# Sparse attention and two gated stages on one core: four of nine transposed score banks split on ScalarE with a subtracting matmul, v of the last keys padded by DMA

## The chip, the core and the metric

The kernel runs on one core of a Trainium2 chip, as one program. The metric is the device time of one execution in microseconds (us); 1231.96 us is the median of three executions (1230.54 to 1233.79).

## What is computed

```python
scores = scale * np.matmul(q, k.transpose(0, 1, 3, 2))      # (4, 8, 576, 576), head size 64
thresh = np.max(scores, axis=-1, keepdims=True) - tau
scores = np.where(scores >= thresh, scores, -1e9)
attn = np.exp(scores - np.max(scores, axis=-1, keepdims=True))
attn = attn / (np.sum(attn, axis=-1, keepdims=True) + 1e-09)
x = np.matmul(attn, v)                 # then tokens x 512: 2304 x 512
g = x @ w_gate
x = (silu(g) * (x @ w_val)) @ w_out    # d_ff 1536
out = ((x @ w1) * (x @ w2) @ w3) @ w_out2   # d_ff 1024
```

All inputs are float32 or float64 (the weights come as 64-bit words and are converted on the chip).

## The kernel before

Every product has float32 accuracy from a faster matmul type: an operand is split into a high part `hi`, rounded to the type fp32r, and a low part `lo` = value − hi, and products of the parts are added up in PSUM. Much of the work of the other engines is the making of these pairs.

**Attention.** Two heads of a batch make a pair; there are 16 pairs, and a pair has nine score tiles of 128 queries by 576 keys (four of each head, and a ninth for the last 64 queries of both). For a tile TensorE makes the scores in an `s_bank` (L428, two such banks), VectorE copies them out negated with a running minimum (L467), ScalarE takes the exponential (L476), GpSimd adds tau to the statistic (L459) and VectorE masks and sums (L486, in place in the tile `P`, from the two SBUF tensors `P` and `E`). Then TensorE transposes the masked scores into a `t_bank` (PSUM, 512 columns, four such banks, shared with all other transposes and the outputs of attention). A pair has ten such banks: four of each head (`it_T`, L523), one for the last queries (`it_lq`, L529) and one for the last keys (`it_kl`, L540). Each is split into hi and lo by `evac_split` before TensorE multiplies it with v (`it_pv`, L565 and L570).

**The split.** `evac_split` takes the next letter of a string for each bank. X: ScalarE copies the bank to hi (L499), and VectorE subtracts hi from the bank (L501). Y: ScalarE copies the bank to an SBUF tile (L512), and GpSimd casts (L99) and subtracts (L102). W: ScalarE copies twice (L512, L516), and GpSimd subtracts (L517). X's second step is put off until the next work item has been issued (`deferred`, emptied by `run_item`).

```python
PATHS, LAST = "XYWYXYWYXY", "XW"     # ten letters, ten banks of a pair; LAST for the last pair
```

**v of the last keys.** `VLZ` holds, for each head of a pair, hi and lo of v for the 64 last keys in the 64 partitions of that head, with zeros in the others. `split_v` fills it for each pair with four small GpSimd operations (L99 and L102 on `VLZ`).

**Order.** `some` takes items of the pair from a list (`main`) between the tiles, about 2.2 items for a tile; the build then places the instructions of each engine by its own model of time, so that the order on an engine isn't that of the code. SyncE issues all transfers, in order.

**After attention.** The first gated stage starts while the last pair is still under way: `x_prep` loads attention's output again (`x_dram`, L770) and the reciprocal sums (`r_dram`, L774), adds on GpSimd (L805), scales on VectorE (L808) and splits (L796, L797). From then on the matmuls of the two gated stages (L814) follow on TensorE until the end. Weights are converted in between (L127 to L156).

Of the kernel before, what the change touches and what calls it, by code (L numbers as in the profile page):

```python
# [24 lines left out]
N_TMP, N_BIG, N_HB, N_TA = 6, 3, 3, 3  # L25
# [4 lines left out]
PATHS, LAST = "XYWYXYWYXY", "XW"  # L30
# [5 lines left out]
def kernel(  # L36
# [47 lines left out]
    ident_r = const.tile([P, P], F32R, name="ident_r")  # L84
    tau_sb = const.tile([P, 1], F32, name="tau_sb")
# [141 lines left out]
    def attention(actx, early, tail):  # L227
# [30 lines left out]
        def load_left(b):  # L258
            qk = ld.tile([P, H, D], F32, tag="qkl", name="qkl", bufs=1)
            vl = wk.tile([P, HP, D], F32, tag="vl", name="vl", bufs=2)  # L260
            nc.sync.dma_start(out=qk[0:64], in_=q[b, :, 512:S, :].rearrange("h p d -> p h d"))
            nc.sync.dma_start(out=qk[64:128], in_=k[b, :, 512:S, :].rearrange("h p d -> p h d"))
            vs = v[b, :, 512:S, :].rearrange("(g e) p d -> e p g d", e=2)
            for e in range(2):
                nc.sync.dma_start(out=vl[64 * e:64 * e + 64], in_=vs[e])
            lraw[b] = (qk, vl)
# [17 lines left out]
        def split_left(b):  # L284
# [11 lines left out]
            lsplit[b] = (qks, vl)  # L296

        def split_v(p):
# [4 lines left out]
            vl = lsplit[p // HP][1]  # L303
            for h in range(2):
                r = slice(64 * h, 64 * h + 64)
                vz = VLZ[r, p % 2, h]
                split_pool(vz[:, 0, :], vz[:, 1, :], vl[r, p % HP, :])
# [187 lines left out]
        def evac_split(hi, lo, bank):  # L495
            path = LAST[path_i[0] % len(LAST)] if in_tail else PATHS[path_i[0] % len(PATHS)]
            path_i[0] += 1
            if path == "X":
# [19 lines left out]

        def it_T(p, h, c):
            bank = t_bank()  # L520
            for t in range(4):
                o = 640 * h + c * P
                nc.tensor.transpose(bank[:, t * P:(t + 1) * P], pbuf[p, t][:, o:o + P], ident)  # L523
            evac_split(AT[h][:, 0, c, 0:512], AT[h][:, 1, c, 0:512], bank)

        def it_lq(p):
            bank = t_bank()
            for c in range(4):
                nc.tensor.transpose(  # L529
                    bank[:, c * P:(c + 1) * P], pbuf[p, 4][:, c * P:(c + 1) * P], ident  # L530
                )
# [5 lines left out]
        def it_kl(p):  # L537
            bank = t_bank()
            for t in range(4):
                nc.tensor.transpose(bank[:, t * P:(t + 1) * P], pbuf[p, t][:, 512:640], ident)  # L540
            evac_split(ATL[:, 0, 0:512], ATL[:, 1, 0:512], bank)
# [196 lines left out]
    nc.vector.tensor_copy(out=ident_r, in_=ident)  # L738

# [363 lines left out]
```

## Time and profile before

| | |
|---|---|
| median of three executions | 1231.96 us |
| the profiled execution: its time, its span | 1231.65 us, 1229.9 us |
| TensorE matmul busy | 1114.0 us (91%) |
| VectorE busy | 788.0 us (64%) |
| ScalarE busy | 563.0 us (46%) |
| GpSimd busy | 604.7 us (49%) |
| mean granted TensorE clock | 0.971 |

PE is TensorE's matmul, PEld its weight load, DVE VectorE, ACT ScalarE, POOL GpSimd, SP SyncE. Busy time is a mean over stages with different limits, so a change to one stage is read in that stage. An "idle before" is the time in which an engine stood ahead of an instruction, with the instruction that ended it.

### The profile page before, as it was taken

To read this page: it belongs to the slowest core of one execution; us is meant where nothing else is said; L and a number is where in the kernel's file an instruction comes from. 1 tells how busy PE (TensorE), PEld (TensorE's weight loads), DVE (VectorE), ACT (ScalarE), POOL (GpSimd) and SP (SyncE) were. 2 spreads that over 40 slices of the span, in tenths; PEclk is the share of its full clock that TensorE was granted. 3 is DMA by queue.
4 is the path that set the end of the run, shared out by engine and by line. 5 is a ranking of instruction groups with operands and counts; after the bars stand their busy time and mean duration, and the time that the engine had idled before them with its cause. 6 is when DMAs were issued, how large, how long until landed. Compare 5 with 4: busy or idle time off the path is not lost.

```text
span 1229.9 us, 16704 instructions
## 1 busy us (share of the span) xinstructions
PE 1114.0 (91%) x5972; PEld 952.0 (77%) x5972; DVE 788.0 (64%) x1303; ACT 563.0 (46%) x1010; POOL 604.7 (49%) x602
## 2 busy tenths in 40 slices
PE   7888878888777845999999999999999999999998
PEld 5877777778666644888888888888877888888886
DVE  7999999999988635756546373548795021432223
ACT  6777667777755522634234242335474241231211
POOL 7999989999975423533323142324342131231110
PEclk9999999999978967999999999999999999999999
DMA  9856656555444544321102021113431010000014
GB/s 203 202 134 148 146 132 149 129 131 133 106 133 134 140 118 131 103 69 52 53 18 69 18 69 52 52 35 103 127 107 58 1 35 1 18 18 1 1 52 103
DMA packets 104370, 107.07 MB, mean 87 GB/s; under 512 B 47328, under 2 KB 78688, under 8 KB 104288
## 3 DMA queue, kind: packets, MB, share of 16 engines
q1 hardware_dynamic: 104288, 106.01, 33.2%
q8 instruction: 47, 0.77, 0.3%
q14 instruction: 35, 0.29, 0.1%
HBM read 68.16 MB, written 14.23 MB: 67 GB/s over the span
## 4 chain that ended last, share of the span: by engine, by line
PE 55%; DVE 15%; POOL 13%; DMA 8%; issue 3%; SPq 3%; ACT 1%; DVEq 0%; POOLq 0%; ACTq 0%
PE t_bank L814 36%; PE s_bank L814 18%; DVE P L486 5%; POOL AT L102 4%; DMA slot<-r_dram 3%; DVE P L467 3%; POOL AT L99 3%; DMA raw<-in_moe_w_gate_dram 2%; POOL AT L517 2%; DMA raw<-in_moe_w_dram 2%; POOL stat L459 2%; SPq L770 1%; DVE tmp L156 1%; DVE slot L797 1%; DVE tmp L144 1%
## 5 line engine op out<-in xcount | busy, mean ns | idle before, releaser
L814 PE MATMUL t_bank<-slot,slot 128*128 128x512 f32 (+1 forms) x2592 | 566.3, 374 | 25.2 <-ACT slot L796 14.1
L814 PEld LDWEIGHTS t_bank<-slot,slot 128*128 128x128 f32 x2592 | 461.4, 191 | 113.2 <-ACT slot L796 14.7
L486 DVE SCALAR_TENSOR_TENSOR P<-P,stat,E 128x576 f32<-128x576 f32 x144 | 184.2, 1303 | 1.6 <-POOL stat L459 1.3
L814 PE MATMUL s_bank<-h,slot 128*128 128x512 f32 (+1 forms) x720 | 163.6, 376 | 16.6 <-POOL h L106 15.6
L149 POOL TENSOR_TENSOR raw<-raw 128x512 int32<-128x512 int32 x76 | 86.9, 1144 | 159.7 <-ACT raw L148 149.2
L814 PEld LDWEIGHTS s_bank<-h,slot 128*128 128x128 f32 x720 | 128.7, 194 | 40.9 <-POOL h L106 16.5
L1043 POOL TENSOR_TENSOR h<-tmp,h 128x512 fp32r<-128x512 f32 (+1 forms) x38 | 45.8, 1204 | 200.5 <-ACT h L1041 200.5
L106 POOL TENSOR_TENSOR h<-tmp,h 128x512 fp32r<-128x512 f32 (+1 forms) x60 | 73.5, 1225 | 136.5 <-ACT h L105 136.4
L1039 DVE TENSOR_TENSOR tmp<-tmp,t_bank 128x512 f32<-128x512 f32 (+1 forms) x40 | 25.3, 633 | 178.3 <-PE t_bank L814 178.3
L476 ACT ACTIVATE E<-P,stat 128x576 f32<-128x576 f32 x144 | 112.6, 789 | 54.6 <-DVE P L467 27.9
L428 PE MATMUL s_bank<-R,L 128*128 128x288 f32 x512 | 100.3, 318 | 28.9 <-DVE P L467 24.8
L467 DVE TENSOR_SCALAR_CACHE_REDUCE P<-s_bank,neg 128x576 f32<-128x576 f32 x144 | 114.0, 806 | 5.1 <-PE s_bank L428 4.9
L899 DVE TENSOR_TENSOR tmp<-tmp,t_bank 128x512 f32<-128x512 f32 (+1 forms) x60 | 37.9, 631 | 116.7 <-PE t_bank L814 112.9
L814 PE MATMUL s_bank<-slot,h 128*128 128x512 f32 x432 | 106.6, 391 | 0.9 <-DVE slot L1029 0.8
L565 PE MATMUL t_bank<-AT,sp 128*128 128x288 f32 x512 | 94.2, 312 | 13.5 <-POOL AT L102 7.9
L428 PEld LDWEIGHTS s_bank<-R,L 128*128 128x128 f32 x512 | 74.9, 193 | 39.1 <-DVE P L467 34.6
L814 PEld LDWEIGHTS s_bank<-slot,h 128*128 128x128 f32 x432 | 80.0, 188 | 18.3 <-DVE slot L1029 2.1
L898 ACT ACTIVATE tmp<-t_bank 128x512 f32<-128x512 f32 (+1 forms) x60 | 33.3, 555 | 128.1 <-PE t_bank L814 125.3
L565 PEld LDWEIGHTS t_bank<-AT,sp 128*128 128x128 f32 x512 | 76.3, 195 | 19.0 <-POOL AT L102 11.2
L861 DVE TENSOR_TENSOR slot<-s_bank,slot 128x1024 f32<-128x1024 f32 (+1 forms) x68 | 77.6, 1142 | 18.6 <-PE s_bank L814 16.5
L523 PE MATMUL t_bank<-ident,P 128*128 128x128 f32 x512 | 75.7, 282 | 10.0 <-ACT AT L516 2.5
L156 DVE SCALAR_TENSOR_TENSOR tmp<-tmp,raw 128x512 f32<-128x512 f32 x76 | 66.6, 876 | 26.6 <-POOL raw L149 26.6
(105 smaller groups left out, 1511.4 us busy)
## 6 DMA issues: line engine op xcount, KB each, us to landing
raw<-in_moe_w_dram SPq DMA_DIRECT2D x32, 512.0 KB
raw<-in_moe_w_out_dram SPq DMA_DIRECT2D x20, 512.0 KB
x_dram<-xs SPq DMA_DIRECT2D x64, 144.0 KB
L<-qhi SPq DMA_DIRECT2D x60, 128.0 KB
L<-qlo SPq DMA_DIRECT2D x60, 128.0 KB
raw<-in_moe_w_gate_dram SPq DMA_DIRECT2D x12, 512.0 KB
raw<-in_moe_w_val_dram SPq DMA_DIRECT2D x12, 512.0 KB
ld<-in_k_dram SPq DMA_DIRECT2D x16, 256.0 KB
```

Of the source, the lines that this page charges most:

```text
L102: nc.gpsimd.tensor_tensor(out=lo, in0=src, in1=f32(hi), op=ALU.subtract)
L106: nc.gpsimd.tensor_tensor(out=lo, in0=src, in1=f32(hi), op=ALU.subtract)
L149: nc.gpsimd.tensor_tensor(out=a, in0=a, in1=x, op=ALU.subtract)
L156: nc.vector.scalar_tensor_tensor(out=f32(m), in0=f32(m), scalar=2.0 ** 20, in1=f32(a), op0=ALU.add, op1=ALU.mult)
L428: nc.tensor.matmul(o, lhsT=lhs, rhs=R[:, c:c + HALF], start=(h == hs2[0] and e == 0), stop=(h == hs2[-1] and e == 1),)
L467: nc.vector.tensor_scalar(out=p_tile(p, i).rearrange("p (a c) -> p a c", a=2), in0=sb[:, :, 0:HALF], scalar1=neg, scalar2=None, op0=ALU.mu ...
L476: nc.scalar.activation(out=e, in_=p_tile(p, i), func=ACTF.Exp, scale=-1.0, bias=stats[p // HP][:, 0, c:c + 1],)
L486: nc.vector.scalar_tensor_tensor(out=t, in0=t, scalar=stats[b][:, 1, c:c + 1], in1=e, op0=ALU.is_le, op1=ALU.mult, accum_out=sums[b][:, c: ...
L523: nc.tensor.transpose(bank[:, t * P:(t + 1) * P], pbuf[p, t][:, o:o + P], ident)
L565: nc.tensor.matmul(o, lhsT=vs[:, 4 * h + c, :, :].rearrange("p a d -> p (a d)"), rhs=AT[h][:, e, c, cs], start=(c == 0 and e == 0), stop=F ...
L814: nc.tensor.matmul(o, lhsT=lhs(a), rhs=rhs(c), start=(first and i == 0), stop=(last and i == 2))
L861: nc.vector.tensor_tensor(out=a, in0=s, in1=a, op=ALU.add)
```

## The change

Three things are changed, all in the attention part.

1. The letters are now nine for ten banks, so that they move round from pair to pair: `"XZYXZZYXZ"`, and `"XZ"` for the last pair. W is gone. Z is new: ScalarE copies the bank to hi; TensorE multiplies hi with minus the identity (`minus_r`) into the same bank, so that the bank then holds value − hi; ScalarE copies the bank to lo. The last two steps are put off until the next item, as X's second step is. In all 160 banks there were 51 X, 72 Y and 37 W; there are now 56 X, 32 Y and 72 Z. The transposes of a bank are issued as one accumulation group (`turn_p`), so that a further matmul can add to it.
2. v of the last keys is split once for a batch into `vls` (two GpSimd operations of 128x256, for four pairs), and two transfers a pair on SyncE's queue move 64 partitions of it into `VLZ`.
3. The pool of extra SBUF tiles for Y has one buffer in place of three (`N_TA`), and the raw v of the last keys one in place of two.

```diff
-N_TMP, N_BIG, N_HB, N_TA = 6, 3, 3, 3
+N_TMP, N_BIG, N_HB, N_TA = 6, 3, 3, 1
-PATHS, LAST = "XYWYXYWYXY", "XW"
+PATHS, LAST = "XZYXZZYXZ", "XZ"
+    minus_r = const.tile([P, P], F32R, name="minus_r")
-            vl = wk.tile([P, HP, D], F32, tag="vl", name="vl", bufs=2)
+            vl = ld.tile([P, HP, D], F32, tag="vl", name="vl", bufs=1)
@@ split_left
-            lsplit[b] = (qks, vl)
+            vls = wk.tile([P, HP, 2, D], F32R, tag="vls", name="vls", bufs=2)
+            split_pool(vls[:, :, 0, :], vls[:, :, 1, :], vl)
+            lsplit[b] = (qks, vls)
@@ split_v
-            vl = lsplit[p // HP][1]
+            vls = lsplit[p // HP][1]
             for h in range(2):
                 r = slice(64 * h, 64 * h + 64)
-                vz = VLZ[r, p % 2, h]
-                split_pool(vz[:, 0, :], vz[:, 1, :], vl[r, p % HP, :])
+                nc.sync.dma_start(out=f32(VLZ[r, p % 2, h]), in_=f32(vls[r, p % HP]))
@@ evac_split
-            if path == "X":
+            if path == "Z":
+                nc.scalar.copy(out=hi, in_=bank)
+
+                def rest():
+                    nc.tensor.matmul(bank, lhsT=minus_r, rhs=hi, start=False, stop=True,
+                                     skip_group_check=True)
+                    nc.scalar.copy(out=lo, in_=bank)
+
+                deferred.append(rest)
+            elif path == "X":
+        def turn_p(bank, parts):
+            for t, part in enumerate(parts):
+                nc.tensor.matmul(
+                    bank[:, t * P:(t + 1) * P], lhsT=part, rhs=ident, is_transpose=True,
+                    start=(t == 0), stop=(t == len(parts) - 1),
+                )
@@ it_T (it_lq and it_kl in the same way)
-            for t in range(4):
-                o = 640 * h + c * P
-                nc.tensor.transpose(bank[:, t * P:(t + 1) * P], pbuf[p, t][:, o:o + P], ident)
+            o = 640 * h + c * P
+            turn_p(bank, [pbuf[p, t][:, o:o + P] for t in range(4)])
+    nc.vector.tensor_scalar(out=minus_r, in0=ident, scalar1=-1.0, scalar2=None, op0=ALU.mult)
```

Line numbers move a little in the changed kernel: L470 is L467 of before, L489 is L486, L431 is L428, L462 is L459, L101 and L104 are L99 and L102, L331 is L328 (transposes of k and q), L534 stands for all transposes of scores, L505 is the new matmul, L824 is L808.

On TensorE, in the second head's part of a pair, before (L523 transposes of scores, L428 the next tiles' scores):

```order
L523 MATMUL t_bank<-ident,P_976 128x128 [waits Activation_49]
L523 MATMUL t_bank<-ident,P_977 128x128
L523 MATMUL t_bank<-ident,P_978 128x128
L523 MATMUL t_bank<-ident,P_979 128x128
L428 MATMUL s_bank<-R,L 128x288 [waits DVE_49]
L428 MATMUL s_bank<-R,L 128x288 x3
L428 MATMUL s_bank<-R,L 128x288 [waits DVE_49]
L428 MATMUL s_bank<-R,L 128x288 x3
```

and with the change, at the like place:

```order
L534 MATMUL t_bank<-ident,P_964 128x128 [waits DVE_49]
L534 MATMUL t_bank<-ident,P_965 128x128
L534 MATMUL t_bank<-ident,P_966 128x128
L534 MATMUL t_bank<-ident,P_967 128x128
L331 MATMUL t_bank<-ident,ld_987 128x128 [waits Activation_49]
L331 MATMUL t_bank<-ident,ld_987 128x128 x3
L534 MATMUL t_bank<-ident,P_964 128x128 [waits DVE_49]
L534 MATMUL t_bank<-ident,P_965 128x128
L534 MATMUL t_bank<-ident,P_966 128x128
L534 MATMUL t_bank<-ident,P_967 128x128
L505 MATMUL t_bank<-AT,minus_r 128x512 [waits Activation_49]
L431 MATMUL s_bank<-R,L 128x288 [waits DVE_49]
```

The subtracting matmul of the first bank comes after two other groups of transposes and ahead of the next scores, and waits there for ScalarE's copy.

On GpSimd, in the middle of attention, about one pair before (`sp` is v of the pair):

```order
L99 TENSOR_SCALAR VLZ<-vl 64x64
L459 TENSOR_SCALAR stat<-stat,tau_sb 128x2
L99 TENSOR_SCALAR AT<-tmp 128x512
L102 TENSOR_TENSOR VLZ<-vl,VLZ 64x64
L102 TENSOR_TENSOR AT<-tmp,AT 128x512
L99 TENSOR_SCALAR sp_2715<-ld_2119 128x8x64
L99 TENSOR_SCALAR VLZ<-vl 64x64
L517 TENSOR_TENSOR AT<-tmp,AT 128x512
L102 TENSOR_TENSOR sp_2715<-ld_2119,sp_2715 128x8x64
L102 TENSOR_TENSOR VLZ<-vl,VLZ 64x64
L99 TENSOR_SCALAR AT<-tmp 128x512
L459 TENSOR_SCALAR stat<-stat,tau_sb 128x2 x2
```

and with the change, from the v of one pair to that of the next:

```order
L101 TENSOR_SCALAR sp_3533<-ld_2958 128x8x64
L104 TENSOR_TENSOR sp_3533<-ld_2958,sp_3533 128x8x64
L101 TENSOR_SCALAR AT<-tmp 128x512
L104 TENSOR_TENSOR AT<-tmp,AT 128x512
L462 TENSOR_SCALAR stat<-stat,tau_sb 128x2 x2
L101 TENSOR_SCALAR AT<-tmp 128x4x2x64
L462 TENSOR_SCALAR stat<-stat,tau_sb 128x1
L104 TENSOR_TENSOR AT<-tmp,AT 128x4x2x64
L462 TENSOR_SCALAR stat<-stat,tau_sb 128x2 x2
L101 TENSOR_SCALAR sp_3829<-ld_3247 128x8x64
L104 TENSOR_TENSOR sp_3829<-ld_3247,sp_3829 128x8x64
```

A whole pair now has two banks on GpSimd, and nothing on `VLZ`.

On VectorE, in the last pair, where the first gated stage's x is prepared, before (L808 scales x with sums that a transfer brings; the row of `P_4524` is the last of this pair's nine L467):

```order
L467 TENSOR_SCALAR P_4523,stat<-s_bank,neg 128x576 [waits PE_49]
L138 TENSOR_SCALAR tmp<-raw 128x512
L467 TENSOR_SCALAR P_4524,stat<-s_bank,neg 128x576 [waits PE_49]
L808 TENSOR_TENSOR tmp<-tmp,slot_4638 128x512 [waits DMAHW5_49,Pool_49]
L141 TENSOR_SCALAR raw<-raw 128x512 [waits DVE_49]
```

and with the change:

```order
L470 TENSOR_SCALAR P_4433,stat<-s_bank,neg 128x576 [waits PE_49]
L824 TENSOR_TENSOR tmp<-tmp,slot_4545 128x512 [waits DMAHW7_49,Pool_49]
L513 TENSOR_TENSOR ATL<-t_bank,ATL 128x512 [waits Activation_49]
L470 TENSOR_SCALAR P_4434,stat<-s_bank,neg 128x576 [waits PE_49]
```

The wait for such a transfer now stands earlier in the last pair, after its third L470.

## Rows read from the trace of the kernel before

**Rows 1.** Busy time by stretch, the whole core; (x) counts instructions.
```profile
core 0: us, PE busy (x) PEld busy (x) DVE busy (x) ACT busy (x) POOL busy (x), PEclk, DMA share, GB/s
0.00:46.00 46.00, 35.71 (x236) 30.69 (x237) 38.75 (x93) 32.00 (x62) 37.07 (x50) 1.00 0.95 207
46.00:309.00 263.00, 220.67 (x1623) 201.56 (x1621) 259.77 (x516) 188.14 (x377) 250.22 (x286) 0.99 0.61 140
309.00:374.00 65.00, 47.48 (x265) 40.91 (x264) 56.46 (x104) 38.67 (x74) 50.38 (x49) 0.84 0.46 116
374.00:480.00 106.00, 68.70 (x316) 55.95 (x316) 65.56 (x85) 45.58 (x79) 49.02 (x40) 0.81 0.50 141
480.00:1230.00 750.00, 741.48 (x3540) 622.90 (x3538) 367.47 (x510) 258.64 (x420) 218.00 (x180) 1.00 0.17 51
575.00:600.00 25.00, 25.00 (x112) 20.71 (x111) 15.45 (x18) 10.71 (x17) 10.14 (x9) 1.00 0.22 64
```
**Rows 2.** Groups by line and form, 46 to 309 us, VectorE's two main ones.
```profile
L486 DVE SCALAR_TENSOR_TENSOR P<-P,stat,E 128x576 f32<-128x576 f32 x110 | 143.8, 1332 | 1.6 <-POOL stat L459 1.3
L467 DVE TENSOR_SCALAR_CACHE_REDUCE P<-s_bank,neg 128x576 f32<-128x576 f32 x109 | 86.2, 805 | 1.8 <-PE s_bank L428 1.7
```
**Rows 3.** Timeline of VectorE and GpSimd, three masks and what GpSimd did beside them.
```profile
110.24 0.81 DVE L486 SCALAR_TENSOR_TENSOR P<-P,stat,E 128x576 f32<-128x576 f32 x1
111.05 0.63 POOL L99 TENSOR_SCALAR AT<-raw 128x512 fp32r<-128x512 f32 x1 [1.35 <-ACT raw L512]
...
124.16 1.26 POOL L102 TENSOR_TENSOR AT<-tmp,AT 128x512 fp32r<-128x512 f32 x1
124.25 1.79 DVE L486 SCALAR_TENSOR_TENSOR P<-P,stat,E 128x576 f32<-128x576 f32 x1
```
**Rows 4.** Groups by line and form, 46 to 309 us: GpSimd's splits.
```profile
L102 POOL TENSOR_TENSOR AT<-tmp,AT 128x512 fp32r<-128x512 f32 x39 | 55.8, 1437 | 0.4
L99 POOL TENSOR_SCALAR AT<-tmp 128x512 fp32r<-128x512 f32 x39 | 29.9, 769 | 1.7 <-ACT tmp L512 1.1
L102 POOL TENSOR_TENSOR AT<-raw,AT 128x512 fp32r<-128x512 f32 x21 | 29.7, 1418 | 0.2
L517 POOL TENSOR_TENSOR AT<-tmp,AT 128x512 fp32r<-128x512 f32 x16 | 22.1, 1378 | 0.2
L99 POOL TENSOR_SCALAR AT<-raw 128x512 fp32r<-128x512 f32 x22 | 17.2, 784 | 1.8 <-ACT raw L512 1.4 <-DMA x_dram<-xs 0.5
L99 POOL TENSOR_SCALAR VLZ<-vl 64x64 fp32r<-64x64 f32 x24 | 13.8, 577 | 1.0
L102 POOL TENSOR_TENSOR VLZ<-vl,VLZ 64x64 fp32r<-64x64 f32 x24 | 12.7, 529 | 1.0
L517 POOL TENSOR_TENSOR AT<-raw,AT 128x512 fp32r<-128x512 f32 x8 | 11.8, 1469 | 0.2
```
**Rows 5.** The same view: a VectorE subtraction of X and a ScalarE copy.
```profile
L512 ACT COPY tmp<-t_bank 128x512 f32<-128x512 f32 x55 | 32.5, 594 | 5.1 <-PE t_bank L523 4.1 <-POOL sp L102 0.5 <-POOL stat L459 0.3
L501 DVE TENSOR_TENSOR AT<-t_bank,AT 128x512 fp32r<-128x512 f32 x25 | 17.0, 679 | 0.0
```
**Rows 6.** Waits, 46 to 309 us: total, times, longest.
```profile
PE s_bank L428 <- DVE P L467: 19.2, 23, 2.8
PE t_bank L565 <- POOL AT L102: 4.7, 5, 1.5
```
**Rows 7.** Chain of waits, piece of an earlier transfer of v of the last keys.
```profile
75.99 2.00 DMA vl<-in_v_dram
```
**Rows 8.** Chain of waits in the last pair: two transfers of the sums.
```profile
347.59 9.68 DMA slot<-r_dram
358.13 14.02 DMA slot<-r_dram
```
**Rows 9.** Groups by line and form, 309 to 374 us.
```profile
L486 DVE SCALAR_TENSOR_TENSOR P<-P,stat,E 128x576 f32<-128x576 f32 x19 | 23.2, 1242 | 0.0
L808 DVE TENSOR_TENSOR tmp<-tmp,slot 128x512 f32<-128x512 f32 x4 | 4.1, 1032 | 8.4 <-DMA slot<-r_dram 8.4
```
**Rows 10.** Timeline of ScalarE and VectorE: the two steps of an X bank.
```profile
127.94 0.58 ACT L499 CAST AT<-t_bank 128x512 fp32r<-128x512 f32 x1
...
130.53 0.68 DVE L501 TENSOR_TENSOR AT<-t_bank,AT 128x512 fp32r<-128x512 f32 x1
```

More of the change, by code (lines that the diff above doesn't have):

```diff
@@ L527, in it_lq @@
             bank = t_bank()
[L528 to L531, printed above, removed]
+            turn_p(bank, [pbuf[p, 4][:, c * P:(c + 1) * P] for c in range(4)])
             evac_split(
@@ L538, in it_kl @@
             bank = t_bank()
-            for t in range(4):
-                nc.tensor.transpose(bank[:, t * P:(t + 1) * P], pbuf[p, t][:, 512:640], ident)
+            turn_p(bank, [pbuf[p, t][:, 512:640] for t in range(4)])
             evac_split(ATL[:, 0, 0:512], ATL[:, 1, 0:512], bank)
```

## The prediction, made before the change was run

> **What bounds the kernel now.** I read the busy time by stretch first [rows 1]. From 480 us to the end TensorE is busy for 741 of 750 us: that half is bound by its matmuls, and nothing of the change is in it. The change acts before 374 us, where attention runs. In the stretch from 46 to 309 us VectorE is busy for 259.8 of 263 us and GpSimd for 250.2, TensorE for 220.7 and ScalarE for 188.1. There are 108 masks (L486) in it by its 110 rows less two at the edges, nine for a pair, so 12 pairs at 21.9 us each. VectorE has no room there: it is the bound.
>
> Next I asked what VectorE spends its time on, by line and form [rows 2]. The minimum over a score bank (L467) takes 805 ns and reads one PSUM operand. The mask (L486) does the same number of elements, from two SBUF operands, and takes 1332 ns on average. The timeline shows why [rows 3]: while GpSimd waits for a ScalarE copy, a mask takes 0.81 us; when one starts 0.09 us after a GpSimd subtraction of 1.26 us it takes 1.79 us, about the rest of the subtraction longer. So a mask has a floor of 0.81 us and otherwise waits for the GpSimd operation that began before it. Over the stretch that wait is 110 x (1.332 - 0.81) = 57 us of VectorE's 260. GpSimd doesn't stand in the chain by its results so much as by being busy.
>
> The Trainium skill, "SBUF — State Buffer", section "Who interferes with whom", says that a VectorE instruction with two SBUF inputs and a GpSimd instruction that reads SBUF exclude each other for a whole instruction, the one that starts first going first. The two durations of the mask agree, and so does L467, which stays at one duration.
>
> **The change, part by part.** All sums are for the stretch of 12 pairs; the two ends follow.
>
> GpSimd loses work. A Y bank costs it 2.21 us: the four Y groups together take 132.6 us for 60 banks [rows 4]. By ten banks a pair and two Y in nine letters, 27 of 60 remain, so 33 x 2.21 = 73 us go. All 24 W subtractions go, 22.1 + 11.8 = 33.9 us. The filling of VLZ goes, 13.8 + 12.7 = 26.5 us. Added are three splits of v for a batch, half as large as a Y bank: 3 x 1.1 = 3.3 us. That is 130 us less, and leaves 120 of 250 us.
>
> VectorE gains by what the mask no longer waits for. I take the wait as proportional to GpSimd's busy share: from 95% to 120 us of a stretch then near 240, 50%. So 57 x (1 - 0.50/0.95) = 27 us go. Added are 4 X subtractions (3.33 instead of 3 a pair) of 679 ns [rows 5], 2.7 us. Net 24 us, and VectorE alone would then allow 263 - 24 = 239 us.
>
> TensorE gets 53 subtracting matmuls (4.44 a pair) of 512 columns. Back to back such matmuls take 25.00 us for 112, or 223 ns [rows 1], so 11.9 us. The transposes stay the same in number. TensorE would be busy for 220.7 + 11.9 = 232.6 us, which is 97% of 239. So it is the next bound. It stands idle for 42 us now. Of these 19.2 us end with L467 giving back a score bank, which a faster VectorE shortens, and 4.7 us end with GpSimd's subtraction, most of which goes [rows 6]. The other 18 us are many small waits for ScalarE, VectorE and transfers. If 13 or 14 of them stay, the stretch takes 246 us. I take 246, between VectorE's 239 and the 263 of no gain, nearer the first because VectorE's wait is measured and only some of TensorE's are certain: **17 us less**.
>
> ScalarE makes 29 copies more (14.4 a pair instead of 12) of 594 ns [rows 5]: 188.1 + 17.4 = 205.5 us of 246. It isn't the bound, and I cost this at nothing; if the stretch came down to 220 us it would be.
>
> The filling of VLZ is now two transfers a pair. A transfer from SBUF to SBUF of this size isn't in the trace; the nearest row is a landing of 2.00 us for v of the last keys [rows 7], and the largest that such a small piece could reach is the 9.68 us of a transfer of the sums among others [rows 8]. Both are less than the half pair (11 us) between the item that issues them and the first use of VLZ in it_pv, so I cost them at nothing; were they late, TensorE would wait at L570. They stand on SyncE's queue among stores of attention's output, and wait there for TensorE's use of VLZ two pairs back, which is over. One buffer instead of three for Y is matched by fewer Y: nothing. The extra copy of minus the identity is one short operation at the start: nothing.
>
> The first 46 us hold two pairs, with GpSimd busy for 37.1 us but transfers at 0.95 of the engines' time [rows 1]. I take 2 us, between 0 (transfers bound it) and 4 (as a pair later, 1.4 us each, and a little over).
>
> The last pairs, 309 to 374 us, wait for transfers. VectorE stands for 8.4 us at L808, and the two transfers behind it take 9.68 and 14.02 us [rows 8, 9]. The mask's excess is 19 x (1.242 - 0.81) = 8.2 us, of which about half goes. But the order puts the wait of L824 after the third minimum of the last pair, where it was after the ninth, so less of the pair can cover it. I take 2 us gained, between a loss of 10 (one transfer more that nothing covers) and a gain of 8. From 374 to 480 us the same work waits for the same transfers and moves up as a whole.
>
> Sum: 17 + 2 + 2 = 21 us. The profiled execution took 1231.65 us, 0.3 us from the median of the three, so the sum holds for both: 1231.65 - 21 = 1210.65, **1211 us**.
>
> **The rivals.**
>
> *TensorE stops at the subtracting matmul, and the kernel gets slower.* Its instructions run in order. Before, no step of a split stood on TensorE; now 72 matmuls wait for ScalarE's hi copy with the next scores behind them, and VectorE behind those. Each needs ScalarE's 594 ns after the transposes plus its queue. If it stops for s at each of the 53, the stretch takes 246 + 53 s: with s = 0.32 us the gain is gone, and with s = 0.6 us, a whole copy, it takes 278 us, 15 more than now. With nothing gained at the ends that is 1231.65 + 15 = **1247 us**. For it: the order puts the next scores right behind the matmul, and ScalarE has exponentials between its copies. Against it: two further groups of transposes stand between a bank and its matmul in the rows shown, about a microsecond of other work.
>
> The same rival has a second form, the banks. An X bank is held from the copy at 127.94 to the subtraction's end at 131.21 us, 3.3 us [rows 10], a Y bank only for one copy. Z is held for a copy, a matmul and another copy with a hand-over between each. Some 18 uses of four banks in 21.9 us allow 4.9 us each on average; above that, TensorE waits for a bank.
>
> The Trainium skill, "PSUM — Partial Sum Buffer", section "PSUM bank collisions raise a hardware error", says that two engines must not touch the same part of a bank at one time. By that rule the three steps of a Z bank can't overlap, which speaks for this form; the X bank's rows show its two steps one after the other too.
>
> *No change.* Either the mask's wait isn't halved, because GpSimd's remaining operations start just when a mask is ready (the add of tau, L459, comes right before it), or TensorE gives back what VectorE gains, s near 0.3 us. Also here belongs that Z's steps only lengthen the chain from a mask to it_pv. About **1231 us**. For it: TensorE at 97% of VectorE's new bound; against it: VectorE's 57 us are on the bound itself.
>
> *All of VectorE's gain arrives.* The small waits of TensorE were only the shadow of VectorE's, the stretch takes 239 us, the start gains 4 and the last pairs 8: 1231.65 - 24 - 4 - 8 = **1196 us**. For it: before, VectorE held 99% beside a GpSimd at 95%, so waits between engines are covered well.
>
> **How the numbers follow.** 0.3%, 3.7 us, is about what a measurement of this kernel can tell from no change. My forecast has 0.60, all of the gain 0.16, no change 0.11, slower 0.13. So faster has 0.76, same 0.11, slower 0.13. The range goes from 1192 us, a little below the third rival, to 1236 us, which takes in the case of no change and a small loss; it leaves out most of the slower rival and a gain at both ends together, under 0.2.
>
> **What would show it.** Right: in the like stretch the mask's mean falls from 1332 to about 1080 ns, GpSimd's busy time is near half of the stretch, TensorE's is over 90%, and a pair takes about 20.5 us. Subtracting matmuls take little idle time before them. Wrong: the mask stays above 1250 ns; or it falls, and yet VectorE shows idle time before L470, with TensorE's idle time ended by ScalarE's copies at L505 (the slower rival), or by ScalarE or VectorE at transposes (the banks). If the stretch shrinks but the end doesn't move, the loss is between the last pair and 480 us, with VectorE waiting at L824.

## The result, and the profile after

The changed kernel takes 1209.80 us (median of four runs, 1208.42 to 1210.93) where the kernel before took 1231.84 us beside it (four runs). The ratio is 0.9819, with a 95% interval of 0.9801 to 0.9838: 22 us less. The profiled execution took 1208.80 us with a span of 1207.0 us, 22.9 us less than before. A second set of five runs, in a later batch, gave 1207.90 us and 0.9789 (0.9776 to 0.9803).

The busy time by stretch, the whole core; the stretches answer to those of [rows 1], and their edges are the same places of the work:

```profile
core 0: us, PE busy (x) PEld busy (x) DVE busy (x) ACT busy (x) POOL busy (x), PEclk, DMA share, GB/s
0.00:46.00 46.00, 36.02 (x233) 30.27 (x234) 38.31 (x95) 33.14 (x63) 25.16 (x37) 1.00 0.85 205
46.00:284.00 238.00, 221.34 (x1636) 203.52 (x1635) 220.78 (x515) 198.69 (x400) 124.69 (x149) 1.00 0.68 156
284.00:345.00 61.00, 50.21 (x330) 43.72 (x328) 55.42 (x112) 46.42 (x89) 32.56 (x31) 0.97 0.59 152
345.00:458.00 113.00, 75.23 (x323) 60.96 (x323) 58.13 (x86) 45.88 (x80) 43.88 (x36) 0.81 0.45 127
458.00:1207.00 749.00, 737.90 (x3528) 619.88 (x3526) 364.64 (x505) 255.72 (x416) 216.04 (x179) 1.00 0.17 51
```

Before, VectorE had 3 us of idle time in the second of these stretches and GpSimd 13; now VectorE has 17, TensorE 17 and GpSimd 113. Counted from mask to mask (the twelve like pairs go from the start of the second pair's last mask to that of the fourteenth's), the time stands so:

| | before | after | difference | predicted |
|---|---|---|---|---|
| to the second pair's last mask | 46.6 | 46.2 | −0.4 | −2 |
| twelve like pairs | 262.0 | 238.0 | −24.0 | −17 |
| from there to the last mask of all (the last two pairs) | 64.5 | 60.4 | −4.1 | −2 |
| from the last mask to the end of the span | 856.7 | 862.4 | +5.7 | 0 |

The whole is as large as predicted. Two of its parts aren't: more came from the like pairs, and some was given back behind attention. How much more depends on the edges. With the next mask as the edge, which is the first one of the third and of the fifteenth pair (53.4 and 314.9 us before, 50.1 and 291.2 after), the four differences are −3.3, −20.3, −5.0 and +5.7 us. So the parts of attention are known to some 4 us only, and the loss behind it is the one that stands either way.

The groups by line and form in the like pairs, 46 to 284 us, answer to [rows 2, 4, 5]:

```profile
L489 DVE SCALAR_TENSOR_TENSOR P<-P,stat,E 128x576 f32<-128x576 f32 x109 | 103.6, 963 | 5.8 <-POOL stat L462 5.6
L470 DVE TENSOR_SCALAR_CACHE_REDUCE P<-s_bank,neg 128x576 f32<-128x576 f32 x108 | 86.5, 808 | 8.4 <-PE s_bank L431 8.4
L513 DVE TENSOR_TENSOR AT<-t_bank,AT 128x512 fp32r<-128x512 f32 x36 | 24.6, 683 | 3.7 <-ACT AT L511 3.7
L505 PE MATMUL t_bank<-AT,minus_r 128*128 128x512 f32 x48 | 21.0, 444 | 0.8 <-ACT AT L502 0.8
L534 PE MATMUL t_bank<-ident,P 128*128 128x128 f32 x471 | 67.0, 274 | 4.0 <-DVE AT L513 2.3 <-ACT ATL L507 0.6 <-DVE klo L337 0.3
L585 PE MATMUL t_bank<-ATL,VLZ 128*128 128x288 f32 x92 | 19.5, 295 | 0.0
L104 POOL TENSOR_TENSOR AT<-tmp,AT 128x512 fp32r<-128x512 f32 x20 | 28.8, 1440 | 1.3
```

The mask fell from 1332 to 963 ns; the minimum, with one PSUM operand, stayed (805, now 808 ns). The subtracting matmul has 0.8 us of idle time before all its 48, and `it_pv`'s product with `VLZ` none. VectorE's idle time ahead of these three of its groups is 17.9 us, where the same groups had 3.4 [rows 2, 5].

The timeline shows that masks and GpSimd's reads still hold each other up where they meet:

```profile
103.92 0.62 POOL L101 TENSOR_SCALAR sp<-ld 128x512 fp32r<-128x512 f32 x1
103.98 1.15 DVE L489 SCALAR_TENSOR_TENSOR P<-P,stat,E 128x576 f32<-128x576 f32 x1 [0.41 <-POOL stat L462]
104.61 1.67 POOL L104 TENSOR_TENSOR sp<-ld,sp 128x512 fp32r<-128x512 f32 x1
105.07 1.83 DVE L489 SCALAR_TENSOR_TENSOR P<-P,stat,E 128x576 f32<-128x576 f32 x1
...
108.81 0.82 DVE L489 SCALAR_TENSOR_TENSOR P<-P,stat,E 128x576 f32<-128x576 f32 x1 [0.42 <-POOL stat L462]
```

The first mask starts 0.06 us after a GpSimd cast and takes 1.15 us; the subtraction that starts beside it takes 1.67 us, where the one of [rows 3] took 1.26; and the mask that starts beside that takes 1.83. The last one shown, before which GpSimd has nothing but tau, takes 0.82.

Between the last pair and the dense second half, the chain of waits (start, us, what) ends with a transfer of weights:

```profile
420.92 10.24 DMA slot<-x_dram
...
436.40 13.14 DMA raw<-in_moe_w_gate_dram
449.54 0.02 issue
449.57 0.04 DVE tmp L140
...
450.39 1.75 DVE tmp L824
452.13 0.61 DVE tmp L915
452.74 0.04 issue
452.79 0.79 PE t_bank L830
```

VectorE takes its instructions in order: L140 waits for the weights, L824 and L915 stand behind it, and TensorE waits 10.0 us for the bank that L915 reads. Before, the same transfer (13.59 us) ended a like wait of 11.8 us, so this alone is no loss.

### The profile page after: what moved, and what is told of

Same layout as the page of the kernel before. It is cut to its first block, busy times and chain, and to the rows that moved or that the text cites. A ratio compares the mean times of both kernels' runs of the same rounds, so it can differ in the third digit from the quotient of the medians.

```text
span 1207.0 us, 16739 instructions
## 1 busy us (share of the span) xinstructions
PE 1120.7 (93%) x6044; PEld 958.3 (79%) x6044; DVE 737.3 (61%) x1309; ACT 579.8 (48%) x1045; POOL 442.3 (37%) x429
## 4 chain that ended last, share of the span: by engine, by line
PE 65%; DVE 15%; DMA 10%; issue 4%; ACT 3%; SPq 2%; POOL 2%; DVEq 0%; ACTq 0%; POOLq 0%
PE t_bank L830 39%; PE s_bank L830 19%; DVE P L489 5%; DVE P L470 4%; PE t_bank L580 3%; DMA raw<-in_moe_w_gate_dram 3%; DMA slot<-r_dram 2%; DMA raw<-in_moe_w_dram 2%; PE s_bank L431 2%; SPq L786 1%; DVE AT L513 1%; PE t_bank L534 1%; ACT E L479 1%; DMA slot<-x_dram 1%; DVE slot L813 1%
## 5 line engine op out<-in xcount | busy, mean ns | idle before, releaser
L830 PE MATMUL t_bank<-slot,slot 128*128 128x512 f32 (+1 forms) x2592 | 566.3, 374 | 21.2 <-DVE tmp L915 10.0
L830 PE MATMUL s_bank<-h,slot 128*128 128x512 f32 (+1 forms) x720 | 166.4, 379 | 9.8 <-POOL h L108 9.1
L489 DVE SCALAR_TENSOR_TENSOR P<-P,stat,E 128x576 f32<-128x576 f32 x144 | 138.4, 974 | 5.9 <-POOL stat L462 5.7
L470 DVE TENSOR_SCALAR_CACHE_REDUCE P<-s_bank,neg 128x576 f32<-128x576 f32 x144 | 115.2, 809 | 14.9 <-PE s_bank L431 14.6
L479 ACT ACTIVATE E<-P,stat 128x576 f32<-128x576 f32 x144 | 114.3, 800 | 20.3 <-DVE P L470 15.8
L431 PE MATMUL s_bank<-R,L 128*128 128x288 f32 x512 | 99.8, 317 | 12.8 <-DVE P L470 10.1
L534 PE MATMUL t_bank<-ident,P 128*128 128x128 f32 x640 | 94.7, 279 | 18.1 <-DVE tmp L915 5.0
L915 DVE TENSOR_TENSOR tmp<-tmp,t_bank 128x512 f32<-128x512 f32 (+1 forms) x60 | 37.9, 632 | 116.8 <-PE t_bank L830 113.1
L534 PEld LDWEIGHTS t_bank<-ident,P 128*128 128x128 f32 x640 | 75.7, 143 | 27.0 <-DVE tmp L915 5.2
L431 PEld LDWEIGHTS s_bank<-R,L 128*128 128x128 f32 x512 | 74.2, 190 | 24.6 <-DVE P L470 20.4
L149 ACT ACTIVATE raw<-raw,ebias 128x512 int32<-128x512 int32 x76 | 58.1, 765 | 59.5 <-DVE tmp L146 43.7
L580 PE MATMUL t_bank<-AT,sp 128*128 128x288 f32 x512 | 81.8, 300 | 2.1 <-DVE AT L513 2.1
```

The costliest lines, as they stand in the source:

```text
L149: nc.scalar.activation(out=a, in_=x, func=ACTF.Relu, scale=8.0, bias=ebias[:, 0:1])
L431: nc.tensor.matmul(o, lhsT=lhs, rhs=R[:, c:c + HALF], start=(h == hs2[0] and e == 0), stop=(h == hs2[-1] and e == 1),)
L470: nc.vector.tensor_scalar(out=p_tile(p, i).rearrange("p (a c) -> p a c", a=2), in0=sb[:, :, 0:HALF], scalar1=neg, scalar2=None, op0=ALU.mu ...
L479: nc.scalar.activation(out=e, in_=p_tile(p, i), func=ACTF.Exp, scale=-1.0, bias=stats[p // HP][:, 0, c:c + 1],)
L489: nc.vector.scalar_tensor_tensor(out=t, in0=t, scalar=stats[b][:, 1, c:c + 1], in1=e, op0=ALU.is_le, op1=ALU.mult, accum_out=sums[b][:, c: ...
L534: nc.tensor.matmul(bank[:, t * P:(t + 1) * P], lhsT=part, rhs=ident, is_transpose=True, start=(t == 0), stop=(t == len(parts) - 1),)
```

## The experiments

**The theory.** The gain comes from GpSimd reading SBUF less, because a mask waits for a GpSimd operation that reads SBUF, and for nothing else of it; what then bounds the like pairs is VectorE and TensorE by turns. The rivals: that what counted was GpSimd's queue (results late, whatever it does); that the gain came from `VLZ` or from the moved order of the work; that TensorE alone is the new bound; and for the end, that Z's longer chain gives back what was lost there.

All ratios are to the kernel before in the same batch, with 95% intervals. "Like pairs" is the time of the twelve pairs, counted as in the table above.

### e1: GpSimd's load given back, by reading

Each Z bank outside the last pair issues a multiplication and an addition on a scratch tile, whose result nobody uses (the tile's allocation is left out of the cut):

```diff
             if path == "Z":
                 nc.scalar.copy(out=hi, in_=bank)
+                if not in_tail:
+                    nc.gpsimd.tensor_scalar(
+                        out=dummy, in0=dummy, scalar1=1.0, scalar2=1.0, op0=ALU.mult, op1=ALU.mult
+                    )
+                    nc.gpsimd.tensor_tensor(out=dummy, in0=dummy, in1=dummy, op=ALU.add)
```

> The changed kernel, with GpSimd work added beside each Z bank outside the last pair: a multiply and an addition over a scratch tile of 128x512 in SBUF, which no other engine reads or waits for. They give GpSimd back about what the change took from it (some 125 us in twelve pairs). Theory A (the gain is that the mask of VectorE no longer meets GpSimd operations that read SBUF): the mask's mean goes back from 963 to 1200 ns or more in the middle stretch, a pair from 19.8 to 21.5 us or more, the whole to 1228 to 1240 us. Rival B (the gain is that hi and lo come out of a shorter chain, without GpSimd's results in it): nothing waits for the added work, so 1208 to 1214 us, mask near 963 ns or dearer without any cost.

Measured: 1231.0 us, ratio 0.9988 (0.997 to 1.0005): the whole gain is gone. The like pairs take 260.2 us. GpSimd is busy for 228.81 of 260 us, with these rows of its groups and of the mask (51 to 311 us):

```profile
L510 POOL TENSOR_TENSOR dummy<-dummy 128x512 f32<-128x512 f32 x53 | 64.9, 1224 | 1.3
L507 POOL TENSOR_SCALAR dummy<-dummy 128x512 f32<-128x512 f32 x53 | 40.6, 766 | 0.7
...
L492 DVE SCALAR_TENSOR_TENSOR P<-P,stat,E 128x576 f32<-128x576 f32 x109 | 121.2, 1135 | 9.3 <-POOL stat L465 9.2
```

The mask rose by 172 ns, less than expected. Over 109 masks that is 19 of the 22 us that the like pairs lost; VectorE's idle time stayed near the changed kernel's (260 − 240.26 = 20 us, and 17 there). So work on GpSimd that reads undoes the change, and it does so through the mask.

### e2: the same load, by writing only

Four memsets of the same scratch tile stand in place of the two operations:

```diff
+                for _ in range(0 if in_tail else 4):
+                    nc.gpsimd.memset(dummy, 0.0)
```

> As the run with added reading work, but the added work is four memsets of the scratch tile for each Z bank, which write SBUF and read nothing. Theory A with reading as the cause: the mask stays below 1000 ns, 1209 to 1216 us. Rival C (what cost time was GpSimd's queue: the add of tau stood behind the splits in it and came late to the mask): as slow as the run with reading work, with VectorE idle before the mask and the add of tau as what ended it, 1225 us or more. Rival B: 1208 to 1214 us.

Measured: 1210.78 us, ratio 0.9826 (0.9812 to 0.9841), which is the changed kernel's. The like pairs take 235.5 us. The same two groups (51 to 287 us):

```profile
L507 POOL MEMSET dummy<- 128x512 f32 x217 | 114.2, 526 | 6.1
...
L492 DVE SCALAR_TENSOR_TENSOR P<-P,stat,E 128x576 f32<-128x576 f32 x110 | 101.3, 939 | 6.9 <-POOL stat L465 6.7
```

GpSimd is busy for 220.62 of 236 us, and it costs nothing: the mask is at 939 ns, not above the changed kernel's. With e1 this settles it: an occupied GpSimd and a full queue of it are harmless here, and reading SBUF is what counts. The Trainium skill, "SBUF — State Buffer", section "Who interferes with whom", states the rule in this form (a VectorE instruction with two SBUF inputs contends with a GpSimd instruction that reads SBUF, not with one that only writes it); both runs agree, 1135 against 939 ns. The timeline of this run says the same mask by mask: counted from the third pair's first mask to the fifteenth's, 57 of 108 masks began during a memset and took 0.81 us in the median, as did the 10 that began beside no GpSimd operation, and the 15 that began during a subtraction took 1.56 us.

### e3 and e4: the two parts alone

`VLZ` by transfers, the letters as before (in the kernel before, with one Y buffer as in the change; the split into `vls` is left out of the cut):

```diff
-                split_pool(vz[:, 0, :], vz[:, 1, :], vl[r, p % HP, :])
+                nc.sync.dma_start(out=f32(VLZ[r, p % 2, h]), in_=f32(vls[r, p % HP]))
```

> The kernel before with the padding of v by transfers alone (and one extra SBUF tile for Y in place of three, which its space needs); letters as before. Theory A: GpSimd loses 26.5 less 3.3 us of 250 in twelve pairs, so the mask's wait of 57 us falls by about a tenth or a little more, 5 to 8 us, and the whole takes 1223 to 1228 us. Rival B: no chain is shortened, 1230 to 1233 us.

Measured: 1227.42 us, ratio 0.9958 (0.9943 to 0.9972). The like pairs take 256.4 us, 5.6 less than before; the mask 1273 ns. That is the first expectation.

The letters with Z, `VLZ` on GpSimd as before (in the changed kernel; the raw v's buffers, as before too, are left out of the cut):

```diff
-                nc.sync.dma_start(out=f32(VLZ[r, p % 2, h]), in_=f32(vls[r, p % HP]))
+                vz = VLZ[r, p % 2, h]
+                split_pool(vz[:, 0, :], vz[:, 1, :], vl[r, p % HP, :])
```

> The changed kernel with the padding of v on GpSimd as before; the letters with Z stay. Theory A: GpSimd is busy for about 150 us of the middle stretch, mask 990 to 1050 ns, 1212 to 1218 us; the two parts add up to the whole gain within 4 us. Rival B: all of the gain is Z's, 1208 to 1212 us.

Measured: 1210.97 us, ratio 0.9821 (0.9805 to 0.9838). The like pairs take 246.4 us, 15.6 less than before; the mask 989 ns. In the like pairs the parts add up, 5.6 + 15.6 = 21.2 of 24.0. Over the whole they don't: the time is the second expectation's and not the first's 1212 to 1218. The letters alone give all of the gain, although their attention ends 7.8 us later than the changed kernel's (352.4 instead of 344.6 us). From the last mask to the end they take 856.1 us and not 862.4. That stretch, which no part of the change means to touch, therefore differs by 6 us between two builds.

### e5: a second matmul for each Z bank

The second matmul adds nothing, by a matrix of zeros (`zero_r`, whose making is left out of the cut):

```diff
-                    nc.tensor.matmul(bank, lhsT=minus_r, rhs=hi, start=False, stop=True,
+                    nc.tensor.matmul(bank, lhsT=minus_r, rhs=hi, start=False, stop=False,
+                                     skip_group_check=True)
+                    nc.tensor.matmul(bank, lhsT=zero_r, rhs=hi, start=False, stop=True,
```

> Each Z bank gets a second matmul of 128x512, with a matrix of zeros, right behind the subtracting one: 72 of them, 53 in the twelve like pairs, and the results stay the same. Back to back such a matmul took 223 ns, so TensorE gets 53 x 0.223 = 11.8 us more in the like pairs (busy 221 -> 233 us of 238) and ScalarE's second copy of each bank starts 0.22 us later. Theory A (after the change VectorE sets the pace with its work plus the hand-overs to its neighbours, and TensorE at 93% still has room): the like pairs stay within 3 us of 238, the time within 1209 to 1214 us. Rival B (TensorE is the bound of the like pairs now, its 17 us of idle time being hand-overs that cannot go): the added time arrives, the like pairs take 248 to 252 us, 1220 to 1226 us. Between them (TensorE and VectorE bind by turns): 242 to 246, 1214 to 1219 us.

Measured: 1213.66 us, ratio 0.9845 (0.9827 to 0.9864). The like pairs take 244.5 us:

```profile
46.00:290.00 244.00, 232.12 (x1705) 213.80 (x1704) 222.92 (x513) 201.70 (x404) 125.65 (x151) 1.00 0.66 150
```

TensorE is busy for 10.8 us more (221.34 before this edit), of which 3.6 to 6.5 us arrive, by which of two profiles of the changed kernel one takes (below). With the first masks of the third and fifteenth pairs as edges it is busy for 8.9 us more (233.64 against 224.72), of which 1.4 to 4.4 arrive. The like pairs are between the two theories, the whole time is still in the first one's range: TensorE at 93% isn't the bound alone, and has little room left.

### e6: no Y at all

```diff
-PATHS, LAST = "XZYXZZYXZ", "XZ"
+PATHS, LAST = "XZZ", "XZ"
```

> No Y: the letters are XZZ, so the 32 Y banks become Z and GpSimd splits no score bank any more; X stays as often. In the like pairs that takes 27 x 2.2 = 60 us of reading work off GpSimd (125 -> 65 us), adds 27 copies of 594 ns on ScalarE (199 -> 215 us of 238) and 27 x 0.223 = 6 us on TensorE (221 -> 227 us). Theory A (the mask's wait still costs VectorE time): the wait falls from 16 to about 8 us, the like pairs take 230 to 234 us, 1202 to 1207 us. Rival B (TensorE is the bound): 6 us longer, 244 us, 1214 to 1219 us. Rival C (ScalarE at 215 us takes over, its two copies of a bank come late): idle time of TensorE before the subtracting matmul and of VectorE before the minimum grows, 1215 us or more.

Measured: 1216.52 us, ratio 0.9869 (0.9846 to 0.9891); the like pairs take 251.3 us. The third expectation is the one that came. In the groups (48 to 300 us) the mask has nearly reached its floor, and the gain is lost at other places:

```profile
L489 DVE SCALAR_TENSOR_TENSOR P<-P,stat,E 128x576 f32<-128x576 f32 x109 | 89.2, 833 | 7.5 <-POOL stat L462 7.5
L470 DVE TENSOR_SCALAR_CACHE_REDUCE P<-s_bank,neg 128x576 f32<-128x576 f32 x107 | 85.6, 811 | 21.2 <-PE s_bank L431 21.1
...
L505 PE MATMUL t_bank<-AT,minus_r 128*128 128x512 f32 x70 | 31.0, 448 | 5.6 <-ACT AT L502 5.5
```

TensorE now stops at the subtracting matmul for ScalarE's copy (5.6 us, and 0.8 in the changed kernel), and VectorE stands for 21 us for scores that come late. This is the prediction's slower rival, at a denser mix of Z than the change has. It is not the whole of it: the stop is 0.08 us for each of the 70, and VectorE also stands for 9.8 us at X's subtraction (L513) for ScalarE's hi, 3.7 in the changed kernel. ScalarE comes late at both places, though it is busy for only 210 of 252 us.

### e7: a third each

```diff
-PATHS, LAST = "XZYXZZYXZ", "XZ"
+PATHS, LAST = "XZYXZYXZY", "XZ"
```

> A third of the banks each for X, Z and Y (XZYXZYXZY): in the like pairs Y goes from 27 to 40 banks and Z from 53 to 40. GpSimd gets 13 x 2.2 = 29 us of reading work more (125 -> 154 us), ScalarE 13 copies less (199 -> 191 us), TensorE 13 x 0.223 = 3 us less (221 -> 218 us). Theory A (the mask's wait is what counts, and it rises with GpSimd's reading work): the wait rises from 16 to about 23 us, the like pairs take 241 to 246 us, 1213 to 1218 us. Rival B (TensorE is the bound): 3 us shorter, 1205 to 1208 us. Rival C (ScalarE's copies set the pace): faster too, 1203 to 1207 us.

Measured: 1206.36 us, ratio 0.9783 (0.9768 to 0.9798). The like pairs take 243.4 us, which is the first theory's 241 to 246; the whole is 3 us shorter than the changed kernel's and not 3 to 8 longer. The last two pairs gain 5 us of it (55.3 us instead of 60.4), or 2 with the fifteenth pair's first mask as the edge (51.5 instead of 53.3).

### e9: five banks of the last pair as W again

```diff
-PATHS, LAST = "XZYXZZYXZ", "XZ"
+PATHS, LAST = "XZYXZZYXZ", "XW"
```

> Only the last pair differs: its five Z banks are W again, as before the change (ScalarE copies twice, GpSimd subtracts: five subtractions of 1.4 us back on GpSimd, no subtracting matmul). The like pairs should stay at 238 us. Attention's last mask came 28.6 us earlier by the change and the kernel's end only 22.9, so 5.7 us were given back between. Theory A (the chain to the first gated stage's matmuls runs over transfers of x and of the weights, whose places in SyncE's order differ from build to build, and not over the way a bank is split): 1205 to 1216 us, with attention's end within 3 us of 344.6 and the difference in waits for transfers. Rival B (the three steps of a Z bank lengthen the tail of the last pair): 4 to 6 us faster, 1204 to 1206 us, by a shorter stretch between the last mask and the dense half.

Measured: 1206.01 us, ratio 0.978 (0.976 to 0.9799). From the last mask to the end it takes 855.1 us, 7.3 less; the last two pairs take 62.1 us, 1.7 more. Both expectations allow the time. Attention's last mask, at 349.9 us, isn't within 3 us of 344.6 as the first one has it, and the stretch behind it is shorter as the second one has it, so the four combinations were run once more in one batch.

### e10 to e13: four combinations side by side

The changed kernel as it is (e10); W in the last pair (e11); a third each (e12); and both (e13):

```diff
-PATHS, LAST = "XZYXZZYXZ", "XZ"
+PATHS, LAST = "XZYXZYXZY", "XW"
```

> The changed kernel as it is, beside the three others of this batch on the same chip: 1208 to 1212 us. A second profile of it shows how far stages scatter from one execution to the next: if the scatter is small, the like pairs take 237 to 239 us again and attention's last mask lies at 344 to 346 us; if the like pairs differ by 2 us or more from 238.0, differences of that size between kernels are no finding.

> Five Z banks of the last pair are W, once more, now beside the changed kernel. Theory A (which way the last pair is split changes nothing by itself; the kernel's end hangs on the places of transfers behind attention): equal to the changed kernel within 0.2%, or a difference whose trace shows it in another transfer at the end of the chain. Rival B (Z's chain lengthens the last pair): 0.3 to 0.5% faster than the changed kernel, with a shorter time of the last two pairs (below 60 us).

> A third of the banks each for X, Z and Y, last pair as in the changed kernel, once more beside it. By its first profile the like pairs took 5 us longer (mask 1.046 instead of 0.963 us) and the whole 2 us less. Theory A (more reading work on GpSimd costs the like pairs 4 to 7 us; what the end gives back differs by the build's order): like pairs 242 to 246 us, whole 1204 to 1209 us. Rival B (the like pairs' difference was scatter): 236 to 240 us.

> Both edits, a third each and W in the last pair: all Y and W together, the least Z. If the two act independently: 1209.8 - 3.4 - 3.8 = 1202.6 us, and it beats all others. If each only shuffles the order of transfers at the end (theory A of both): anything from 1202 to 1210 us, not the sum; like pairs 242 to 246 us as with a third each alone.

| | us, median | ratio to before | like pairs | the same, edges one mask later | last two pairs | last mask to end |
|---|---|---|---|---|---|---|
| as changed | 1207.90 | 0.9789 (0.9776 to 0.9803) | 240.9 | 244.1 | 60.6 | 860.9 |
| W in the last pair | 1204.79 | 0.9769 (0.975 to 0.9789) | 238.8 | 241.5 | 62.1 | 853.7 |
| a third each | 1204.88 | 0.9775 (0.9761 to 0.9788) | 244.7 | 245.2 | 54.7 | 858.7 |
| both | 1209.68 | 0.9816 (0.98 to 0.9831) | 243.4 | 244.0 | 56.4 | 861.9 |

The same program's like pairs take 238.0 us in one profile and 240.9 in the other, so a difference under 3 us there is no finding. These 3 us stand in the fifth of the twelve pairs (20.8 and 23.4 us), where VectorE waits 3.0 us for scores in the one profile and 5.6 in the other. With that, the third of each is slower in the like pairs by these edges (243.4 to 244.7 us in three profiles; 238.0 to 240.9 in the four with the change's letters), as the first theory says. With edges one mask later the two sets meet (243.9 to 245.2 and 241.1 to 244.1), so only the longer mask (1054 ns) is sure. The whole isn't slower. And the two edits don't add: each alone is 3 us below the changed kernel, both together 2 us above it. The changed kernel missed its expected 1208 us by 0.1; W alone is 0.26% faster than it, between its two theories, and its last two pairs aren't shorter, against the second. W in the last pair shortens the stretch behind the last mask by 6 to 7 us beside one set of letters, and lengthens it by 2 to 3 beside the other. So it isn't the way of splitting by itself that counts there. What differs is, for one, the end of the chain of transfers: in the changed kernel its last long piece is w_gate's 13.1 us (above), with W in the last pair it is the sums (`r_dram`),

```profile
409.92 10.30 DMA slot<-x_dram
...
425.41 11.75 DMA slot<-x_dram
...
444.32 15.38 DMA slot<-r_dram
```

and with both edits the sums too, later:

```profile
422.26 10.74 DMA slot<-x_dram
...
448.82 16.17 DMA slot<-r_dram
```

Such a transfer takes 10 to 16 us there, and which one is the last, and when it starts, goes with the build. But the end of the chain alone can't be the cause: with W in the last pair it is over later (459.7 us) than in the changed kernel (449.5), and that version is the faster one. More stands right behind the last mask. There the changed kernel's VectorE waits for a transfer of w_out, L915 stands behind it, and TensorE's transposes of the last pair stand behind that:

```profile
351.15 0.43 DVE L140 TENSOR_SCALAR tmp<-raw 128x512 int32<-128x512 int32 x1 [3.58 <-DMA raw<-in_moe_w_out_dram]
351.49 0.68 DVE L915 TENSOR_TENSOR tmp<-tmp,t_bank 128x512 f32<-128x512 f32 x1
...
352.23 0.69 PE L534 MATMUL t_bank<-ident,P 128*128 128x128 f32 x2 [4.96 <-DVE tmp L915]
```

In its second profile this wait of TensorE is 5.3 us; with W in the last pair (e9, e11) it isn't there. It is the largest part of the 6 to 8 us by which TensorE's idle time behind the last mask differs (49.0 and 47.0 us as changed, 40.8 in e11). No run moved one transfer alone, so that the transfers' places make the differences of 3 to 8 us is argued and not shown. The two best versions are 3 us (0.3%) below the changed kernel, with intervals that overlap its own; I call neither better.

## Why the prediction was right

**The sum** was 21 us, and the medians say 22 (25 in the second batch). The mechanism is the one predicted, and e1 against e2 shows it. Two of its terms were mis-sized, in opposite directions: the like pairs gave more (20 to 24 us in place of 17), and behind attention 5.7 us went that were put at nothing. That the sum came out within 2 us is in that part luck.

**GpSimd's busy time** was put at about 120 us of a stretch near 240: 124.69 of 238, right.

**The mask's wait** was to fall by 27 us, "proportional to GpSimd's busy share". It fell from 57 to 109 x (0.963 − 0.81) = 17 us, by 40. This step failed in its size. Its relation, over the kernels run (share from the windows, mask from its group):

| | GpSimd busy share, like pairs | mask, ns | by proportion |
|---|---|---|---|
| before | 95% | 1332 | 1332 |
| `VLZ` by transfers alone | 93% | 1273 | 1321 |
| load given back by reading | 88% | 1135 | 1293 |
| a third each | 64% | 1054 | 1162 |
| Z alone | 58% | 989 | 1129 |
| as changed | 52% | 963 | 1096 |
| no Y | 28% | 833 | 964 |
| load given back by writing, memsets left out | 45% | 939 | 1057 |

The last column is 810 + 522 x share/95%. Every one lies below it by 48 to 158 ns, and with 28% the wait is nearly nil: it falls faster than the share. One reason may be seen in the changed kernel's waits: GpSimd itself waits for VectorE.

```profile
POOL stat L462 <- DVE P L470: 68.4, 33, 4.1
```

It then adds tau and, having nothing queued, leaves the mask alone. That this is the whole reason wasn't shown.

**VectorE's bound** of 239 us came out as the stretch's 238, but not in that way. VectorE's work fell to 220.78 us, and 17 us of idle time came in between, for scores, for the statistic and for ScalarE's hi of an X bank. I had let the bound stand for busy time alone.

**TensorE** was to get 11.9 us of matmuls and be busy for 232.6. It was busy for 221.34, hardly more than before's 220.67. The matmuls are there (53, mean 444 and 430 ns with their overlap), but the stretch holds only 13 records more than before's, because its edges don't cut the two kernels' matmuls at the same places. With the first masks of the third and the fifteenth pair as edges there are 45 more, and L565 and L580 are as many (384), as are L570 and L585 (96):

```profile
53.36:314.85 261.49, 220.24 (x1620) 201.28 (x1619) 258.26 (x512) 187.32 (x377) 248.63 (x284) 0.99 0.60 139
50.10:291.24 241.14, 224.72 (x1665) 207.12 (x1664) 220.59 (x515) 200.05 (x405) 126.07 (x151) 1.00 0.68 154
```

So TensorE's busy time rose by 4.5 us, where 11.9 were predicted, and the other matmuls of the stretch took some 7 us less than before. Why isn't settled. Of the 42 us of TensorE's idle time 17 stayed, where I had put 13 to 14. That the stretch lies near the bound of both engines was right, as e5 shows for TensorE (a load that arrives by a sixth to three fifths) and e7 and e12 for VectorE, less surely (busy for 8 to 10 us more, by a longer mask, of which at most 7 us arrive).

**X's four more subtractions** were right: 40 of 683 ns. **ScalarE**, at 198.69 us of 238, is not the bound, as said, but it is near: in e6 it is what stops TensorE. The prediction's bound for it was its busy time (a stretch of 220 us); it fails sooner, when its copies come late for TensorE's order. **`VLZ` by transfers** was costed at nothing, and L585 has no idle time before any of its 92. **One buffer for Y** was costed at nothing; ScalarE's copy L524 waits for no GpSimd instruction in any row of the waits.

**The start** was to give 2 us and gave 0.4 (3.3 with the edge one mask later): the transfers' share there is still 0.85 (0.95 before). **The last pairs** gave 4.1 (5.0) instead of 2. The wait before L824 moved ahead in the pair, as the order showed, and got shorter: 2.1 us where [rows 9] have 8.4. Behind the last mask the same line waits longer for the sums than before, 12.1 us in place of 9.2.

**"Moves as a whole"** failed: from the last mask to the end 5.7 us were given back (4.2 in the second profile). TensorE's idle time there grew from 46.1 to 49.0 us; the rest is busy time. The step took it that the work behind the last mask waits for the same transfers as before, and it doesn't: the 5.0 us behind w_out's transfer (above) are new. The stretch takes 853.7 to 864.0 us over all the builds, and its 5.7 us are within that spread; that the spread comes from how the transfers of x, sums and weights fall is argued above and not shown.

**The rivals.** That TensorE stops at the subtracting matmul: s was 0.02 us (0.8 / 48), far from the 0.32 that would have eaten the gain, since other transposes and scores stand between; e6 shows the mechanism where Z is denser. Its second form, the banks, hardly shows: L534 has 4.0 us of idle time before it (5.1 before the change, at L523), of which 2.3 end with X's subtraction and 0.6 with a Z bank's second copy (L507). No change: the mask's wait fell more than was needed. All of VectorE's gain: the like pairs did come near its 239 us (238 or 241 by the edges), and the ends gave 4.5 to 8.3 of its 12, but 5.7 us were lost behind them.

## What to carry to other kernels

Where a VectorE operation with two SBUF operands has two durations, look at what GpSimd reads beside it: take reading work off GpSimd, leave it what only writes, and expect the wait to fall faster than GpSimd's busy share. A subtraction that an accumulating matmul with minus the identity can do in the bank cost TensorE here some 0.2 us for 512 columns and ScalarE a second copy (0.60 us), and little else, as long as the build put other matmuls between ScalarE's first copy and it. And a saving ahead of a stretch that hangs on transfers arrives with an error of some microseconds either way, so two versions are compared stage by stage and several builds of a kind side by side, not by one end time.

## What was not expected of the hardware

The mutual wait goes both ways: a GpSimd subtraction that begins during a mask is lengthened as well (1.67 us against 1.26), so each side passes the delay on. In the like pairs of before, 37 subtractions of 128x512 that began during a mask took 1.64 us on average, the other 61 took 1.28. 217 memsets of 128x512 on GpSimd (526 ns each) left the mask at 939 ns, while 106 operations that read brought it to 1135. And with 53 subtracting matmuls TensorE's busy time rose by 4.5 us, where 53 more behind them raised it by 8.9 (edges at the pairs' first masks).
